# Eight neighbour subtractions from VectorE to GpSimd, and a new order of the engines, in an attention and channel-mix kernel

## The chip, the core and the metric

The kernel runs on one core of a Trainium2 chip. A core has five engines that work at the same time, each through its own list of instructions in order: TensorE (PE, matrix products into the accumulation memory PSUM), VectorE (DVE), ScalarE (ACT), GpSimd (POOL) and SyncE (SP, which here only issues transfers). PEld is the load of weights into TensorE. Engines wait for each other through semaphores. Transfers (DMA) between the main memory and the core's working memory SBUF are issued by POOL, SP or ACT and run on 16 DMA engines.

The metric is the device time of one execution in microseconds (us), the median of several runs.

## The reference

Two stages follow each other. The first is attention with a sliding window of 128 positions and a bias that falls with distance, for 8 batches, 8 heads, 576 positions and head size 64. The second is a channel mix in which each token is blended with its neighbour to the left:

```python
rel = pos[:, None] - pos[None, :]
mask = (rel >= 0) & (rel < 128)
scores = np.where(mask, scale * q @ k.T + bias, -1e9)
attn = softmax(scores);  x = attn @ v           # heads side by side: (8, 576, 512)

x_prev = x shifted by one position, 0 at the start
xk = mu_k * x + (1 - mu_k) * x_prev
xr = mu_r * x + (1 - mu_r) * x_prev
k = np.maximum(xk @ w_k, 0)                     # 512 -> 1024
v = k * k @ w_v                                 # 1024 -> 512
r = 1 / (1 + np.exp(-(xr @ w_r)))               # 512 -> 512
out = r * v
```

The kernel computes xk as mu_k * (x - x_prev) + x_prev, and xr likewise with mu_r. The subtraction x - x_prev is the neighbour-token subtraction.

## The kernel before, in words

**Attention.** Batches come one after the other, and each batch has four groups g of two heads. Batch 0 is treated apart and in two parts (positions 0 to 255 and 256 to 575), so that the channel mix can begin early. Later batches are loaded with q and k in a form that VectorE transposes (line 1157, into qt); TensorE makes the scores on 32-row tiles (line 1190), ScalarE the exponential (line 1211), VectorE multiplies by the mask (line 1224), and TensorE multiplies by v (line 803). VectorE takes the reciprocal of the sums (line 809) and scales (line 814, into xu). The result is turned so that channels lie on partitions: for batches 0 to 3 by TensorE (line 841) with a copy on ScalarE (line 717, into xt), for batches 4 to 7 by a transposing transfer from SP (`out_flip`).

**The shift.** The function `shift` works on xt, which has zeros ahead of the first column, so that the neighbour is the same tile one column to the left. For each batch and group it puts three instructions on VectorE: the subtraction into dl (line 867), then two mixes on line 874, which multiply dl by mu and add the neighbour, into xk and xr. There are two dl buffers, so at most two subtractions are open at a time. The first part of batch 0 uses other buffers and lets its xr come later (argument `late`).

**The channel mix.** Two batches form a pair P of 1152 columns, cut into pieces of 256, 256, 384 and 256 columns (first pair) or 512, 384 and 256. For each piece TensorE makes xk @ w_k (line 956), ScalarE the relu (line 963), ScalarE or VectorE the square (lines 927 and 929), TensorE xr @ w_r (line 974), ScalarE a tanh that stands for the sigmoid (line 981), TensorE kk @ w_v (line 990), and VectorE the final product into ot (line 995). A piece needs xk of all four groups of its columns.

**Loads.** Nearly all loads are issued by POOL, in one fixed order: v, weights, the rest of batch 0, batch 1, then batches 2 to 7 (raw for q and k on line 568, vs and tv for v on lines 547 and 552). POOL computes only an iota, two selects and two tiny copies (lines 481, 489, 492, 660).

**What sets the order.** The program is first built as a graph of nodes, each with an engine, a cost in us and the nodes that it waits for. `Plan.run` then plays the graph through: whenever an engine is free, it takes the ready node with the smallest key. The sequence that comes out is the order in which each engine's instructions are written down, and the chip follows it whatever the real durations are. The function `rank` makes the keys: a node of attention gets (4 * batch + group) * 4.7, one of the channel mix the TensorE time planned ahead of it, and both get an offset from the table NUDGE, which has a number for about a thousand nodes, by the order in which they were created. DMA issues have their own number as key and are chained to the issue before. Operations with two possible engines (a square, for one) go to whichever is free first in the plan. The cost of a subtraction in the plan is `dve_t(n, 2)`, (n/2 + 66)/960 us for n columns.

Of the kernel before, what the change touches and what calls it, by code (L numbers as in the profile page):

```python
# [182 lines left out]
def kernel(  # L183
# [12 lines left out]
    nc = tc.nc  # L196
# [26 lines left out]
    BIAS = ()  # L223
    FIN = 384
# [102 lines left out]
    def dve_t(n, fast=1):  # L327
        return (n / fast + 66) / 960.0
# [103 lines left out]
    def rank(prio, need, free):  # L432
        nudge = NUDGE.get(len(plan.nodes), 0.0)
        if prio[0] == 0:
            _, b, part, g = prio[:4]
# [860 lines left out]
```

## Time and profile before

| | |
|---|---|
| median of 3 runs | 227.17 us (226.61 to 227.76) |
| the profiled execution | 226.8 us |
| its span, from the first to the last instruction | 225.0 us |
| PE busy | 215.5 us (96%) |
| VectorE busy | 195.3 us (87%) |
| ScalarE busy | 167.9 us (75%) |
| GpSimd busy | 58.5 us (26%) |
| subtractions of 128x256, 128x320 and 128x576 | 4, 4 and 28, of 290, 318 and 448 ns |
| granted TensorE clock | 0.999 |

Busy time is the time in which an engine had an instruction under way. TensorE's matmuls are pipelined and their ends are modelled, so 96% does not mean that it ran at its peak. An instruction's duration is from its start to its end, and on VectorE the next one often starts before that end; the distance between starts is then the better measure of what an instruction takes from the engine. A chain that ended last is followed back from the last instruction: at each step to what released it, or to the instruction ahead of it on its engine.

### The profile page before, as it was taken

The numbers are of one execution on the slowest core, as the hardware profiler recorded it, in microseconds if no ns is written. First come the engines' busy times: TensorE is split into PE (matmuls) and PEld (weight loads), VectorE is DVE, ScalarE is ACT, GpSimd is POOL, SyncE is SP. The second block draws the span as 40 slices with busy tenths as digits, with TensorE's granted clock in tenths as the row PEclk, the third lists the DMA queues.
The fourth block names the chain that finished last, engine by engine and source line by source line (L and its number), as shares of the span: only waits on it lengthen the run. The fifth ranks groups of instructions, "written<-read, shape, count | busy, mean of one in ns | idle before, by whom it ended". The sixth has DMA issues, their size and how long they took to land.

```text
span 225.0 us, 5805 instructions
## 1 busy us (share of the span) xinstructions
PE 215.5 (96%) x2309; PEld 128.5 (57%) x2339; DVE 195.3 (87%) x378; ACT 167.9 (75%) x319; POOL 58.5 (26%) x88
## 2 busy tenths in 40 slices
PE   8999978999999999999999999999999999999994
PEld 8575736656755555464774545445674455456642
DVE  7387999999999999999998999999999966993432
ACT  3669999498998689967996997676996884527511
POOL 8758535456101900070005600190000000000000
PEclk9999999999999999999999999999999999999999
DMA  6999999999981996189354993599871315141023
GB/s 162 187 166 200 195 155 207 191 189 188 232 166 50 97 209 154 50 56 145 115 69 45 249 188 84 134 153 186 151 108 29 144 47 117 33 144 62 0 93 140
DMA packets 66298, 29.74 MB, mean 132 GB/s; under 512 B 53976, under 2 KB 58336, under 8 KB 66272
## 3 DMA queue, kind: packets, MB, share of 16 engines
q0 software_dynamic: 46832, 16.26, 66.6%
q1 hardware_dynamic: 17696, 12.53, 19.9%
q10 hardware_dynamic: 1744, 0.59, 1.1%
q8 instruction: 18, 0.29, 0.5%
q14 instruction: 8, 0.07, 0.1%
HBM read 33.56 MB, written 9.44 MB: 191 GB/s over the span
## 4 chain that ended last, share of the span: by engine, by line
PE 88%; DVE 3%; ACT 3%; DMA 3%; issue 1%; SPq 1%; DVEq 0%; ACTq 0%
PE uno L990 27%; PE uno L956 27%; PE uno L974 13%; PE duo L803 7%; PE duo L1190 6%; DMA qx<-in_q_dram 3%; PE uno L841 2%; PE uno L708 1%; PE duo L734 1%; PE uno L803 1%; DVE qt L1157 1%; PE duo L747 1%; SPq L581 1%; ACT rl L963 1%; DVE xk L874 1%
## 5 line engine op out<-in xcount | busy, mean ns | idle before, releaser
L956 PE MATMUL uno<-xk,wk_sb 128*128 128x256 bf16 (+2 forms) x410 | 70.4, 313 | 1.2 <-ACT rs L981 0.3
L990 PE MATMUL uno<-wv_sb,kk 128*128 128x512 bf16 (+2 forms) x281 | 67.1, 373 | 1.2 <-issue 0.6
L1211 ACT ACTIVATE at<-duo 128x1024 bf16<-128x1024 f32 x56 | 55.2, 1040 | 13.6 <-PE duo L1190 13.5
L963 ACT ACTIVATE rl<-uno 128x256 bf16<-128x256 f32 (+2 forms) x104 | 47.0, 478 | 12.2 <-PE uno L956 10.9
L956 PEld LDWEIGHTS <-wk_sb 128*128 128x128 bf16 x416 | 38.8, 98 | 22.8 <-issue 1.8
L990 PEld LDWEIGHTS <-kk 128*128 128x128 bf16 x296 | 27.0, 98 | 29.9 <-issue 2.3
L1224 DVE TENSOR_TENSOR at<-at,mask 128x1024 bf16<-128x1024 bf16 x56 | 37.1, 685 | 1.4 <-ACT at L1211 1.2
L547 POOL DMA_DIRECT2D vs<-in_v_dram x32 | 28.5, 905 | 36.4 <-PE duo L803 29.0
L974 PE MATMUL uno<-wr_sb,xr 128*128 128x512 bf16 x135 | 35.1, 379 | 0.5
L927 ACT ACTIVATE kk<-rl 128x256 bf16<-128x256 bf16 (+2 forms) x74 | 35.1, 517 | 0.5
L1157 DVE STREAM_TRANSPOSE qt<-raw 128x576 f32<-128x576 f32 x28 | 33.4, 1236 | 0.0
L981 ACT ACTIVATE rs<-uno 128x512 bf16<-128x512 f32 x36 | 21.6, 616 | 14.0 <-PE uno L974 13.9
L995 DVE SCALAR_TENSOR_TENSOR ot<-rs,uno 128x512 f32<-128x512 bf16 (+2 forms) x37 | 24.2, 664 | 7.6 <-ACT rs L981 4.6
L874 DVE SCALAR_TENSOR_TENSOR xr<-dl,mu_sb,xt 128x576 bf16<-128x576 bf16 (+1 forms) x32 | 24.6, 771 | 0.1
L874 DVE SCALAR_TENSOR_TENSOR xk<-dl,mu_sb,xt 128x576 bf16<-128x576 bf16 (+1 forms) x32 | 24.5, 776 | 0.1
L803 PEld LDWEIGHTS <-at 128*128 128x128 bf16 x576 | 21.4, 98 | 4.9 <-issue 0.8
L814 DVE TENSOR_TENSOR xu<-duo,rc 128x640 bf16<-128x640 f32 x28 | 22.7, 817 | 0.5 <-PE uno L841 0.3
L974 PEld LDWEIGHTS <-xr 128*128 128x128 bf16 x144 | 13.5, 98 | 14.5 <-issue 0.4
L1190 PE MATMUL duo<-qt 32*128 32x256 bf16 (+2 forms) x560 | 18.1, 250 | 1.1 <-ACT at L1211 0.9
L803 PE MATMUL duo<-vs,at 128*128 128x65 bf16 x448 | 18.8, 194 | 0.3 <-ACT at L1211 0.3
L1190 PEld LDWEIGHTS <-qt 32*128 32x128 bf16 x560 | 11.7, 92 | 11.7 <-issue 9.4
L929 DVE TENSOR_TENSOR kk<-rl 128x256 bf16<-128x256 bf16 (+2 forms) x30 | 10.0, 337 | 8.5 <-ACT rl L963 8.0
(73 smaller groups left out, 159.6 us busy)
## 6 DMA issues: line engine op xcount, KB each, us to landing
out_dram<-ot SPq DMA_DIRECT2D x34, 256.0 KB, 2.5
vs<-in_v_dram POOLq DMA_DIRECT2D x32, 128.0 KB, 9.5
raw<-in_q_dram POOLq DMA_DIRECT2D x14, 288.0 KB, 8.8
raw<-in_k_dram POOLq DMA_DIRECT2D x14, 288.0 KB, 9.3
wk_sb<-in_moe_w_k_dram POOLq DMA_DIRECT2D x2, 512.0 KB, 7.8
wv_sb<-in_moe_w_v_dram POOLq DMA_DIRECT2D x2, 512.0 KB, 11.5
qx<-in_k_dram ACTq DMA_DIRECT2D x4, 128.0 KB, 5.1
qx<-in_q_dram SPq DMA_DIRECT2D x4, 128.0 KB, 4.8
```

What stands on the lines that cost most here:

```text
L547: return dma(POOL, 256, issue_t(1024), lambda e: nc.gpsimd.dma_start(out=vs_buf[h.idx][:, j, :, 0:D], in_=v[b, :, 128 * j:128 * j + 128].r ...
L803: nc.tensor.matmul(a[:, hl, t - t0], lhsT=at[:, lo:lo + 128], rhs=vs[:, u, 2 * g + hl, :] if u < NF else tvb[:, 2 * g + hl], start=(u == u ...
L874: lambda e: nc.vector.scalar_tensor_tensor(out=buf[hk.idx][:, g, e0 + c0:e0 + c1], in0=dls(), scalar=mu[:, g:g + 1], in1=xc(1), op0=ALU.mu ...
L927: nc.scalar.activation(out=out, in_=in_, func=AF.Square)
L956: nc.tensor.matmul(one(hp)[:, 0:n], lhsT=wk_sb[:, po, 128 * fo:128 * fo + 128], rhs=xk_buf[hx.idx][:, po, c0:c1], start=(po == 0), stop=(p ...
L963: a = op(ACT, act_t(n), [s], pr, lambda e, hp=hp, hr=hr: nc.scalar.activation(out=rl_buf[hr.idx][:, 0:n], in_=one(hp)[:, 0:n], func=AF.Rel ...
L974: nc.tensor.matmul(one(hp), lhsT=xr_buf[hx.idx][:, po, 128 * c:128 * c + 128], rhs=wr_sb[:, po], start=(po == 0), stop=(po == NPO - 1))
L990: nc.tensor.matmul(one(hv)[:, a:b], lhsT=kk_buf[hk.idx][:, fo, o:o + 128], rhs=wv_sb[:, fo, a:b], start=(fo == 0), stop=(fo == NFO - 1))
L1157: nc.vector.transpose(out=qt_buf[hq.idx][:, S * i:S * i + S].rearrange("p s t -> p (s t)").bitcast(FP32) .rearrange("p (q t) -> p t q", t=TB),
L1190: nc.tensor.matmul(two(hps[j // 2])[:, j % 2, c0:c0 + n], lhsT=qt[r:r + 32, S + 128 * u:S + 128 * u + 128, t], rhs=qt[r:r + 32, q0:q0 + n, t],
L1211: lambda e, ah=ah, j=j: nc.scalar.activation(out=ah(), in_=two(hps[j]), func=AF.Exp, scale=float(scale)), (), [hps[j]])
L1224: nc.vector.tensor_tensor(out=a, in0=a, in1=m, op=ALU.mult)
```

## The change

The subtraction gets a choice of engine. For the second part of batch 0 (four groups of 320 columns) and for batch 1 (four groups of 576 columns) it goes to GpSimd, with a planned cost of 0.0016 us for a column and 0.2 us more. The first part of batch 0 and batches 2 to 7 stay on VectorE. The keys that `rank` gives now include one for GpSimd, equal to TensorE's. The table NUDGE is another one from end to end, with about as many entries, so the order on every engine, and the engine of the squares, can differ throughout.

```diff
+    XPOOL = (0, 1)
...
     NUDGE = {
-        647: 9.44, 648: 14.18, 650: 28.28, 651: -0.02, 652: 28.26, 654: 14.18, 655: 14.18, 656: -0.02, 657: 4.7, 658: 23.5, 659: 14.12, 660: 9.48,
...
+        1914: 2.42, 1916: 1.54, 1918: 18.57, 1923: 0.24, 1925: 18.1,
     }
...
-    def rank(prio, need, free):
+    def keys_of(prio, need, free):
         nudge = NUDGE.get(len(plan.nodes), 0.0)
...
         return {e: (1e9,) + tuple(prio) for e in LEAD}
+
+    def rank(prio, need, free):
+        d = keys_of(prio, need, free)
+        d[POOL] = d[PE]
+        return d
...
         prev = last.get(("xt", b, g))
         last["xt", b, g] = deps[0]
-        d = op(DVE, dve_t(n, 2), list(deps) + [prev], prio + (1, 0),
-               lambda e: nc.vector.tensor_tensor(
+        on = POOL if late is None and b in XPOOL else DVE
+        d = op(on, 0.0016 * n + 0.2 if on == POOL else dve_t(n, 2), list(deps) + [prev], prio + (1, 0),
+               lambda e: (nc.gpsimd if on == POOL else nc.vector).tensor_tensor(
             out=dls(), in0=xc(0), in1=xc(1), op=ALU.subtract), [hd], [ht])
```

148 rows, old and new, of the table NUDGE are left out of this document.

## The prediction

> **What bounds the kernel now.** I read the page of the profile first (shares and the chain), then the table by stretches of 7.5 us, then the chain in order of time, then the groups by shape.
>
> ```profile
> span 225.0 us, 5805 instructions
> PE 215.5 (96%) x2309; PEld 128.5 (57%) x2339; DVE 195.3 (87%) x378; ACT 167.9 (75%) x319; POOL 58.5 (26%) x88
> PE 88%; DVE 3%; ACT 3%; DMA 3%; issue 1%; SPq 1%; DVEq 0%; ACTq 0%
> ```
>
> TensorE is the bound over the whole span, and VectorE holds only 3% of the chain that ended last, about 7 us. Those 7 us have a place. In the next table the columns are the stretch, its length, then for each engine busy us and instructions, the granted clock, the DMA share and GB/s.
>
> ```profile
> 15.00:22.50 7.50, 6.79 (x142) 4.05 (x142) 6.23 (x19) 7.15 (x21) 4.71 (x8) 1.00 1.51 188
> 22.50:30.00 7.50, 6.97 (x108) 4.99 (x107) 7.36 (x16) 7.41 (x18) 3.47 (x5) 1.00 1.49 187
> 30.00:37.50 7.50, 6.13 (x89) 4.10 (x90) 7.50 (x15) 7.43 (x15) 3.87 (x6) 1.00 1.79 178
> 37.50:45.00 7.50, 7.11 (x104) 4.90 (x105) 7.13 (x17) 4.51 (x10) 3.58 (x6) 1.00 1.42 196
> 45.00:52.50 7.50, 7.45 (x80) 4.22 (x80) 7.50 (x12) 5.88 (x11) 4.49 (x6) 1.00 1.71 194
> 52.50:60.00 7.50, 7.50 (x81) 5.29 (x79) 7.43 (x14) 7.50 (x21) 1.87 (x4) 1.00 1.78 208
> 105.00:112.50 7.50, 7.40 (x109) 5.10 (x110) 7.50 (x16) 7.32 (x16) 0.00 (x0) 1.00 0.28 91
> ```
>
> From 15 to 45 us PE is idle for 0.71 + 0.53 + 1.37 + 0.39 = 3.0 us, and VectorE is full from 22.5 us on, ScalarE from 15 to 37.5 us. In the three later rows PE has at most 0.10 us idle, although VectorE stays full. So a microsecond of VectorE is worth something to the end only between about 22 and 45 us, and afterwards only where a VectorE result arrives just in time.
>
> The chain in order of time (start, length, what) shows that stretch:
>
> ```profile
> 27.99 1.02 DVE xu L814 x2
> 29.25 1.17 DVE qt L1157
> ...
> 31.34 0.68 DVE at L1224
> 32.02 1.17 DVE qt L1157
> 33.34 0.45 DVE xr L874
> 33.79 0.94 DVE xk L874 x2
> 34.77 0.83 PE uno L956 x6
> ```
>
> From 27.99 to 34.77 us the chain runs on VectorE nearly without a break and ends in the last xk of batch 0, for which the matmuls of line 956 wait. The break before 33.34 is the subtraction's (33.03 us, below).
>
> **The change part by part.** *Part 1, removed from VectorE.* The eight subtractions that move are the four of 128x320 and the first four of 128x576 on line 867. VectorE's timeline (start, length) has them here:
>
> ```profile
> 24.12 0.33 DVE L867 TENSOR_TENSOR dl<-xt 128x320 bf16<-128x320 bf16 x1
> 24.48 0.55 DVE L874 SCALAR_TENSOR_TENSOR xr<-dl,mu_sb,xt 128x320 bf16<-128x320 bf16 x1
> 33.03 0.31 DVE L867 TENSOR_TENSOR dl<-xt 128x320 bf16<-128x320 bf16 x1
> 33.27 0.52 DVE L874 SCALAR_TENSOR_TENSOR xr<-dl,mu_sb,xt 128x320 bf16<-128x320 bf16 x1
> 43.79 0.44 DVE L867 TENSOR_TENSOR dl<-xt 128x576 bf16<-128x576 bf16 x1
> 44.15 0.82 DVE L814 TENSOR_TENSOR xu<-duo,rc 128x640 bf16<-128x640 f32 x1
> 50.25 0.82 DVE L867 TENSOR_TENSOR dl<-xt 128x576 bf16<-128x576 bf16 x2
> 50.99 1.54 DVE L874 SCALAR_TENSOR_TENSOR xk<-dl,mu_sb,xt 128x576 bf16<-128x576 bf16 x2
> ```
>
> Instructions overlap their neighbour, so what one costs is the distance to the next start: 0.36 us at 24.12, 0.24 us at 33.03, 0.36 us at 43.79, and 0.37 us each for the two at 50.25. I take 0.27 us for each small one (4 x 0.27 = 1.1 us, between 24 and 33.3 us, in the starved stretch) and 0.37 us for each large one (4 x 0.37 = 1.5 us, between 43.8 and 51 us). Of the 1.1 us I count 0.8: ScalarE is as full there (7.41 and 7.43 of 7.5 us) and takes a part of the bound. Ends: 0 and 1.1. Of the 1.5 us I count 0.5. Line 956 turns to batch 1 at 52.59 us, right behind the last xk at 50.99 + 1.54 = 52.53 us, so VectorE is just in time there, but PE shows no wait. Ends: 0 and 1.5.
>
> ```profile
> 52.59 3.52 PE L956 MATMUL uno<-xk,wk_sb 128*128 128x384 bf16 x24
> ```
>
> *Part 2, added to GpSimd.* No two-input operation of GpSimd is in the trace. The nearest rows are these (busy us, mean ns):
>
> ```profile
> L492 POOL TENSOR_SCALAR_AFFINE_SELECT dist<-dist 128x128 bf16<-128x128 bf16 x1 | 0.4, 367 | 0.0
> L660 POOL COPY gap<-xt 1x4 bf16<-1x4 bf16 x2 | 0.4, 178 | 37.5 <-DMA xt<-xu 37.5
> L481 POOL IOTA dist<- 128x256 bf16 x1 | 0.3, 344 | 0.4 <-POOLq L1280 0.4
> ```
>
> Between the copy of 4 elements (178 ns) and the select of 128 (367 ns) lie 1.5 ns for an element. That gives 0.65 us for 320 elements and 1.04 us for 576, in all 6.8 us. Ends: the iota's slope, (344 - 178)/252 = 0.66 ns, gives 0.39 and 0.56 us, in all 3.8 us; twice the select's slope, because there are two inputs, gives 1.1 and 1.9 us, in all 12 us. I take the middle, since the select is the nearest in kind. GpSimd has 2.8 to 4 us idle in each of the stretches concerned, so the work fits. [...]
>
> *Part 3, the new waits.* GpSimd's queue now waits for ScalarE's copy of xt, and behind it stand DMA issues; VectorE's xr and xk now wait for GpSimd. A ready subtraction goes ahead of a ready DMA issue in the planner's order, as its key is smaller. The tightest transfer is the last raw load of batch 2:
>
> ```profile
> 34.44 0.53 POOL L568 DMA_DIRECT2D raw<-in_k_dram  x1 [0.86 <-PE duo L1190]
> 44.89 1.25 DVE L1157 STREAM_TRANSPOSE qt<-raw 128x576 f32<-128x576 f32 x1
> raw<-in_k_dram POOLq DMA_DIRECT2D x14, 288.0 KB, 9.3
> ```
>
> Issued at 34.44 and landing 9.3 us later, it is there at 43.7 us, 1.1 us before the first transpose of that batch at 44.89 us. The four small subtractions put 2.6 us into GpSimd's queue before it. The queue idles 0.86 us before this issue and as long before most others, so I count nothing; if that cover fails, the transpose starts up to 1.5 us late. One subtraction is slower by 0.65 - 0.27 = 0.4 us in its own path to xr and xk, but starts as soon as xt is there rather than behind other VectorE work (the one at 33.03 had waited behind a transpose): nothing counted.
>
> *Part 4, the two engines disturb each other.* The trace shows GpSimd holding VectorE up in one place:
>
> ```profile
> 2.22 1.96 POOL L547 DMA_DIRECT2D vs<-in_v_dram  x2
> L687 DVE COPY dist<-dist 128x192 bf16<-128x192 bf16 x1 | 0.6, 620 | 0.0
> L687 DVE COPY dist<-dist 128x64 bf16<-128x64 bf16 x1 | 0.5, 524 | 0.0
> L687 DVE COPY dist<-dist 128x256 bf16<-128x256 bf16 x1 | 0.2, 214 | 0.0
> L1224 DVE TENSOR_TENSOR at<-at,mask x56: 666/684/693, 31.3 to 183.4; 128x1024 bf16<-128x1024 bf16 x56
> L874 DVE SCALAR_TENSOR_TENSOR xr<-dl,mu_sb,xt x32: 521/812/819, 24.5 to 199.7; 128x576 bf16<-128x576 bf16 x28, 128x320 bf16<-128x320 bf16 x4
> 22.50:45.00 22.50, 3.93 (x8) 1.00 1.57 187
> 22.50:45.00 22.50, 5.16 (x8) 1.00 1.57 187
> ```
>
> Copies of 192 and 64 columns took 620 and 524 ns while a GpSimd instruction ran, although 256 columns take 214 ns. The mask products of line 1224 have two inputs in SBUF and never took more than 693 ns, but GpSimd had only DMA issues then. So the price of a GpSimd subtraction to VectorE is unknown: at the low end 0, at the high end its whole duration. The last two rows are VectorE's busy time from 22.5 to 45 us on line 874 and on line 1224 alone: operations with two SBUF inputs fill (3.93 + 5.16)/22.5 = 40% of it. With an operation hit at a random moment of the 0.65 us, the delay is about 0.15 us each, 0.6 us for the four in the starved stretch. I take 0.6; the ends are 0 and 2.6 us.
>
> *Part 5, the new order.* The table NUDGE is other throughout, so every engine's list changes. What it can gain is what PE idles: of the 3.0 us, parts 1 and 4 leave 2.5. What it can lose has no row of its own; the bound is to pay the starved stretch's largest idle, 1.37 us, once more in a place that is now dense, with some loss in the small gaps: 2 us. I take a gain of 0.7, under a third of what is left, because VectorE and ScalarE are both full there and reordering moves, but doesn't remove, their work. Ends: 2.5 gained, 2 lost.
>
> **Sum.** 0.8 + 0.5 - 0.6 + 0.7 = 1.4 us gained. The profiled execution took 226.8 us (span 225.0), so 225.4 by its own time; the median of the three runs is 227.17, 0.4 above it: 225.8 us. Ends by the terms: 1.1 + 1.5 + 2.5 = 5.1 gained, or 2.6 + 1.5 + 2 = 6.1 lost.
>
> **The rivals.** *Slower: GpSimd holds VectorE for its whole duration.* Place: the stretch from 24 to 35 us, and 43 to 52 us. Each subtraction then takes 0.65 or 1.04 us from VectorE where it took 0.27 or 0.37. The four small ones lose 2.6 - 1.1 = 1.5 us in the starved stretch, the large ones 4.2 - 1.5 = 2.7 us, of which a third, as in part 1, reaches PE: 0.9. Without a gain by order: 227.17 + 2.4 = 229.6; with it 228.9. It decides from a delay of 0.27 us for each small one. For it: the copies above. Against it: the other operations had no such row. [...] The stretched copies agree with a lock, at 620 and 524 ns; for two-input operations no row here tests it.)
>
> *Slower: the order packs PE worse after 45 us.* The idle there is at most 0.10 us in the rows shown, so it has more to lose than to gain; a loss of 1.4 to 2 us eats the gain of part 1: 227.9 to 228.5.
>
> *No change: PE sets the end anyway.* If the relieved time of VectorE is taken by ScalarE's fullness, or given back as waits in the dense part, the time is 227.2.
>
> *Much faster: the order fills the starved stretch.* All of 3.0 us idle and 0.5 of part 1: 223.7.
>
> **How the numbers follow.** Forecast (225.8, its own range 224.8 to 226.0) 0.34; much faster 0.12; no change 0.20; the lock 0.20; the worse order 0.14. A time within 0.5% (1.1 us) of before is about what a measurement can't tell from no change: faster 0.46, same 0.20, slower 0.34. The range reaches from 222.8, the fast case with one more of part 1's microseconds, to 229.7, which takes in the lock's case at the middle price; the longer subtractions (12 us in all) lie beyond it.
>
> **What would show it.** Part 1: 24 subtractions of 128x576 left on VectorE and none of 128x320. Part 2: GpSimd rows on line 867's successor near 0.65 and 1.04 us. Part 4: xr, xk and at rows whose longest is far above 819 and 693 ns, each beside a GpSimd subtraction. Part 5: PE's busy time from 15 to 45 us above 27.0 of 30 us, and from 45 us on as dense as now. Part 3: a wait of qt for a raw load near 44 us, or of xk for GpSimd. The forecast is wrong if the starved stretch doesn't get denser, or if it does and the dense part loses as much.

## The result, and the profile after

The changed kernel takes 245.24 us (median of 4 runs, 244.53 to 246.23) where the kernel before takes 227.12 us (4 runs, 226.61 to 227.76). The ratio is 1.080, with a 95% interval of 1.077 to 1.084: 18.1 us slower, where 1.4 us faster was forecast and the range ended at 229.7 us.

The head of its page and the shares of its chain:

```profile
span 244.4 us, 5821 instructions
PE 219.6 (90%) x2309; PEld 130.6 (53%) x2339; DVE 202.4 (83%) x390; ACT 162.1 (66%) x299; POOL 67.2 (28%) x96
...
PE 71%; DMA 15%; DVE 7%; issue 3%; ACT 3%; POOL 1%; DVEq 0%; POOLq 0%; ACTq 0%; SPq 0%
```

TensorE's share of the chain fell from 88% to 71%, and transfers rose from 3% to 15%. GpSimd itself holds 1%. The table by stretches (columns as in the prediction) has the place:

```profile
15.00:22.50 7.50, 7.20 (x140) 4.24 (x128) 6.40 (x20) 7.22 (x19) 4.81 (x8) 1.00 1.64 179
22.50:30.00 7.50, 5.39 (x95) 4.20 (x94) 4.49 (x9) 7.29 (x18) 3.80 (x5) 1.00 1.47 194
30.00:37.50 7.50, 0.06 (x1) 0.06 (x2) 1.14 (x3) 0.00 (x0) 4.72 (x8) 0.52 1.85 180
37.50:45.00 7.50, 4.83 (x62) 2.73 (x67) 5.79 (x10) 5.81 (x8) 4.86 (x7) 0.79 1.41 196
45.00:52.50 7.50, 4.18 (x53) 2.93 (x43) 5.29 (x11) 3.12 (x5) 1.79 (x3) 0.66 1.77 175
52.50:60.00 7.50, 7.45 (x94) 5.47 (x93) 5.74 (x10) 3.83 (x10) 1.15 (x1) 0.88 0.25 64
```

From 30 to 37.5 us TensorE, VectorE and ScalarE all stand nearly still. TensorE's busy time times its clock, as a rough measure of its progress, is 13.2 us between 30 and 60 us (0.06 x 0.52 + 4.83 x 0.79 + 4.18 x 0.66 + 7.45 x 0.88), against 28.2 us before. With the two rows above (0.4 us gained, then 1.6 us lost) that is 16.2 of the 19.4 us by which the span grew. The table of waits (engine, tile, line, what released it: us in total, times, longest) names the chain of causes:

```profile
DVE xk L875 <- POOL dl L868: 12.1, 3, 8.7
PE uno L841 <- DVE xu L814: 9.5, 1, 9.5
```

VectorE's mix xk waits 8.7 us in one piece for a subtraction, and TensorE 9.5 us for the xu that stands behind that wait in VectorE's list. VectorE's timeline and TensorE's first row after the gap:

```profile
27.36 0.27 DVE L809 RECIPROCAL rc<-uno 128x6 f32<-128x6 f32 x2
36.37 0.55 DVE L875 SCALAR_TENSOR_TENSOR xk<-dl,mu_sb,xt 128x320 bf16<-128x320 bf16 x1 [8.73 <-POOL dl L868]
36.84 0.55 DVE L814 TENSOR_TENSOR xu<-uno,rc 128x384 bf16<-128x384 f32 x1
...
37.44 0.50 PE L841 MATMUL uno<-ident,xu 128*128 128x128 bf16 x3 [9.52 <-DVE xu L814]
```

Why was the subtraction so late? Two of them run together at 34.93 us, and this xk needs the second, which ends at 34.93 + 1.40 = 36.33 us. Their operands, ScalarE's copies into xt, were there at 24.5 and 26.7 us, 10 and 9 us before they ran. ScalarE's rows, and then GpSimd's timeline, which answers (the bracket is the idle time before, and what ended it):

```profile
24.08 0.42 ACT L717 COPY xt<-uno 128x320 bf16<-128x320 bf16 x1
...
26.23 0.46 ACT L717 COPY xt<-uno 128x320 bf16<-128x320 bf16 x1
```

```profile
19.09 0.75 POOL L572 DMA_DIRECT2D wr_sb<-in_moe_w_r_dram  x1 [0.69 <-DMA vs<-in_v_dram]
20.01 1.77 POOL L547 DMA_DIRECT2D vs<-in_v_dram  x2 [0.18 <-issue]
22.35 0.88 POOL L547 DMA_DIRECT2D vs<-in_v_dram  x1 [0.57 <-DMA wk_sb<-in_moe_w_k_dram]
23.75 0.88 POOL L547 DMA_DIRECT2D vs<-in_v_dram  x1 [0.53 <-DMA raw<-in_q_dram]
25.40 0.70 POOL L552 DMA_DIRECT2D tv<-in_v_dram  x1 [0.78 <-DMA raw<-in_k_dram]
26.60 0.76 POOL L572 DMA_DIRECT2D wv_sb<-in_moe_w_v_dram  x1 [0.50 <-DMA raw<-in_q_dram]
27.97 0.74 POOL L572 DMA_DIRECT2D wv_sb<-in_moe_w_v_dram  x1 [0.60 <-DMA raw<-in_k_dram]
30.77 0.54 POOL L568 DMA_DIRECT2D raw<-in_q_dram  x1 [2.06 <-DMA wr_sb<-in_moe_w_r_dram]
31.95 0.54 POOL L568 DMA_DIRECT2D raw<-in_k_dram  x1 [0.63 <-DMA vs<-in_v_dram]
32.83 0.53 POOL L568 DMA_DIRECT2D raw<-in_q_dram  x1 [0.35 <-DMA vs<-in_v_dram]
34.38 0.53 POOL L568 DMA_DIRECT2D raw<-in_k_dram  x1 [1.01 <-DMA vs<-in_v_dram]
34.93 1.40 POOL L868 TENSOR_TENSOR dl<-xt 128x320 bf16<-128x320 bf16 x2
```

Count back from the issue at 30.77: the issue eight places earlier is that of wr_sb at 19.09, and its landing, 11.1 us after the issue and so at 30.2 us, is what the wait ended with. The next three wait for vs loads, again eight places back. In this trace no issue on GpSimd's queue starts before the eighth issue ahead of it has landed (71 of its 79 issues have eight ahead of them). The kernel's own plan knows nothing of that: it starts the four raw issues between 22.2 and 23.9 us and the first two subtractions at 24.5 and 26.7 us, and so they are written behind them. On the chip the first ran at 34.93 us, 10.4 us later than planned. In the kernel before the same queue was as late (the prediction shows its last raw issue at 34.44 us), but it carried only loads there, and no engine's result.

### The profile page after: what moved, and what is told of

The parts are those of the page before. It is cut to its first block, busy times and chain, and to the rows that moved or that the text cites. A ratio compares the mean times of both kernels' runs of the same rounds, so it can differ in the third digit from the quotient of the medians.

```text
span 244.4 us, 5821 instructions
## 1 busy us (share of the span) xinstructions
PE 219.6 (90%) x2309; PEld 130.6 (53%) x2339; DVE 202.4 (83%) x390; ACT 162.1 (66%) x299; POOL 67.2 (28%) x96
## 3 DMA queue, kind: packets, MB, share of 16 engines
q1 hardware_dynamic: 17696, 12.53, 18.1%
## 4 chain that ended last, share of the span: by engine, by line
PE 71%; DMA 15%; DVE 7%; issue 3%; ACT 3%; POOL 1%; DVEq 0%; POOLq 0%; ACTq 0%; SPq 0%
PE uno L991 23%; PE uno L957 21%; PE uno L975 11%; PE duo L803 6%; PE duo L1191 5%; DMA vs<-in_v_dram 5%; DMA raw<-in_k_dram 5%; DMA wk_sb<-in_moe_w_k_dram 3%; PE uno L708 2%; DMA xt<-xu 2%; DVE xk L875 2%; DVE xu L814 1%; PE uno L841 1%; DVE ot L996 1%; DVE qt L1158 1%
## 5 line engine op out<-in xcount | busy, mean ns | idle before, releaser
L957 PE MATMUL uno<-xk,wk_sb 128*128 128x256 bf16 (+2 forms) x413 | 71.8, 315 | 4.4 <-DVE xk L875 3.3
L991 PE MATMUL uno<-wv_sb,kk 128*128 128x512 bf16 (+2 forms) x280 | 68.1, 376 | 1.5 <-issue 1.0
L957 PEld LDWEIGHTS <-wk_sb 128*128 128x128 bf16 x416 | 38.8, 98 | 28.2 <-issue 6.3
L1225 DVE TENSOR_TENSOR at<-at,mask 128x1024 bf16<-128x1024 bf16 x56 | 38.0, 698 | 0.3
L975 PE MATMUL uno<-wr_sb,xr 128*128 128x512 bf16 x133 | 36.3, 385 | 0.8 <-issue 0.2
L875 DVE SCALAR_TENSOR_TENSOR xk<-dl,mu_sb,xt 128x576 bf16<-128x576 bf16 (+1 forms) x32 | 25.7, 802 | 12.3 <-POOL dl L868 12.1
L928 ACT ACTIVATE kk<-rl 128x256 bf16<-128x256 bf16 (+2 forms) x59 | 27.5, 495 | 0.4
L803 PEld LDWEIGHTS <-at 128*128 128x128 bf16 x576 | 22.3, 100 | 6.3 <-issue 2.8
L930 DVE TENSOR_TENSOR kk<-rl 128x256 bf16<-128x256 bf16 (+2 forms) x45 | 15.2, 347 | 10.0 <-ACT rl L964 9.7
L717 ACT COPY xt<-uno 128x576 bf16<-128x576 bf16 (+2 forms) x20 | 10.8, 544 | 16.7 <-PE uno L841 16.7
L803 PE MATMUL duo<-vs,at 128*128 128x65 bf16 x448 | 19.6, 197 | 1.4 <-DVE xu L814 1.2
```

Of the source, the lines that this page charges most:

```text
L803: nc.tensor.matmul(a[:, hl, t - t0], lhsT=at[:, lo:lo + 128], rhs=vs[:, u, 2 * g + hl, :] if u < NF else tvb[:, 2 * g + hl], start=(u == u ...
L875: lambda e: nc.vector.scalar_tensor_tensor(out=buf[hk.idx][:, g, e0 + c0:e0 + c1], in0=dls(), scalar=mu[:, g:g + 1], in1=xc(1), op0=ALU.mu ...
L928: nc.scalar.activation(out=out, in_=in_, func=AF.Square)
L957: nc.tensor.matmul(one(hp)[:, 0:n], lhsT=wk_sb[:, po, 128 * fo:128 * fo + 128], rhs=xk_buf[hx.idx][:, po, c0:c1], start=(po == 0), stop=(p ...
L975: nc.tensor.matmul(one(hp), lhsT=xr_buf[hx.idx][:, po, 128 * c:128 * c + 128], rhs=wr_sb[:, po], start=(po == 0), stop=(po == NPO - 1))
L991: nc.tensor.matmul(one(hv)[:, a:b], lhsT=kk_buf[hk.idx][:, fo, o:o + 128], rhs=wv_sb[:, fo, a:b], start=(fo == 0), stop=(fo == NFO - 1))
```

## The experiments

The theory: the subtractions stand in GpSimd's list behind issues that wait for landings, and what waits for them stands in order on VectorE and TensorE. The rivals: the new order alone; the lock between GpSimd and VectorE; the clock, which is 0.52 in the idle stretch; GpSimd's longer operations. Beside these runs the kernel before took 226.6 to 226.7 us; the ratios are against it.

**The order and the engine apart.** The new order with the subtractions issued on VectorE:

```diff
-               lambda e: (nc.gpsimd if on == POOL else nc.vector).tensor_tensor(
+               lambda e: nc.vector.tensor_tensor(
```

> The new order kept on every engine, only the eight subtractions run on VectorE, at the place in the order that the plan gave them. Theory 1, the queue: the time went because a subtraction stands on GpSimd behind transfer issues that wait, and VectorE and then TensorE wait for it; then 227 to 231 us, with no idle stretch of TensorE near 30 to 37 us. Rival, the order: the new table is bad by itself; then 240 us or more. Rival, the lock (a GpSimd subtraction holds VectorE up for its whole duration): the lock goes too, so this run reads like theory 1; the next two tell them apart.

Measured: 232.54 us, ratio 1.027 (1.023 to 1.031), 1.5 us above what was expected if the queue were the whole cause, and far below the 240 us of the order as the cause. So 5.9 us are lost by the order without any work on GpSimd. By busy time times clock TensorE is 2.6 us behind the kernel before at 37.5 us, 3.7 at 60, 4.0 at 165 and 4.9 at 172.5. Most of it falls in the starved stretch, which the new order made worse; here TensorE waits for ScalarE's exponentials (what held these up was not followed):

```profile
30.00:37.50 7.50, 4.60 (x76) 2.92 (x77) 7.50 (x15) 5.96 (x10) 3.62 (x6) 0.88 1.88 180
...
PE duo L1191 <- ACT at L1212: 3.6, 2, 2.5
```

And the order before, with the eight subtractions on GpSimd at their old places:

```diff
-               lambda e: nc.vector.tensor_tensor(
+               lambda e: (nc.gpsimd if late is None and b < 2 else nc.vector).tensor_tensor(
```

> The order of before kept on every engine, only the eight subtractions run on GpSimd, at the place in the order where they were. Theory 1, the queue: the first subtraction, with its xt ready near 24 us, stands behind two or three raw issues of batch 2, which went out from 30.6 us on, and VectorE waits about 7 to 9 us for it at 24.5 us; 236 to 245 us. Rival, the order: 226 to 228 us. Rival, the lock: the eight subtractions cost about 1 us each where they meet an operation with two SBUF inputs, less 2.5 us saved; 228 to 231 us.

Measured: 241.77 us, 1.066 (1.063 to 1.069). The engine alone costs 15 us in the old order, and 245.24 - 232.54 = 12.7 us in the new one (12.1 by the ratios, since the kernel before took 227.12 us on the one occasion and 226.61 on the other). So 5.9 and 15 us do not add up to 18.1 us. Both fall in the same stretch, which would explain it; that was not shown.

**One instruction.** Of the eight, only the first 128x320 one goes to GpSimd, in the old order (node 730 is its number in the plan):

```diff
-               lambda e: nc.vector.tensor_tensor(
+               lambda e: (nc.gpsimd if e == POOL else nc.vector).tensor_tensor(
...
-                n.emit(n.eng)
+                n.emit(POOL if n.seq == 730 else n.eng)
```

> The kernel before, with one instruction moved: the first subtraction of 128x320 (xt ready near 24 us) runs on GpSimd, at its old place in the order, which is behind three raw issues of batch 2; no other subtraction moves. Theory, the queue: it runs near 33.6 us, VectorE stands at the mix behind it from about 24.5 us, and this one instruction of 0.3 us costs 7 to 10 us: 234 to 237 us. Rival, the lock: at most 1 us: 226 to 228 us.

Measured: 238.61 us, 1.053 (1.048 to 1.058), 1.6 us above the expected range. One instruction, which ran 0.73 us, costs 12 us. GpSimd, and then VectorE:

```profile
32.77 0.53 POOL L568 DMA_DIRECT2D raw<-in_q_dram  x1 [0.86 <-DMA vs<-in_v_dram]
33.31 0.73 POOL L867 TENSOR_TENSOR dl<-xt 128x320 bf16<-128x320 bf16 x1
...
34.08 0.55 DVE L874 SCALAR_TENSOR_TENSOR xr<-dl,mu_sb,xt 128x320 bf16<-128x320 bf16 x1 [10.55 <-POOL dl L867]
```

A wait of 10.55 us is 14 times the 0.73 us that the instruction ran, so neither its duration nor VectorE held for all of that duration makes it up. The xr that stood at 24.48 us in the kernel before now starts at 34.08 us.

The four of batch 1 alone, in the old order:

```diff
-               lambda e: nc.vector.tensor_tensor(
+               lambda e: (nc.gpsimd if b == 1 else nc.vector).tensor_tensor(
```

> The kernel before, with only the four subtractions of batch 1 on GpSimd, at their old places in the order. There the first stands behind a vs issue that went out at 48.45 us, its xt ready at 43.8 us, its mix due at 47.4 us. Theory, the queue: a wait of 2 to 4 us on VectorE, partly covered by TensorE's other work: 227.5 to 231 us. Rival, the lock: four times 0.9 us on VectorE, less 1.5 us saved: 227 to 229 us; it is told by mixes and mask products of 1.6 us or more without an idle VectorE.

Measured: 235.12 us, 1.037 (1.033 to 1.042), 4 us above the expected range. It is the same kind of wait at another place, behind loads of v:

```profile
49.08 0.89 POOL L547 DMA_DIRECT2D vs<-in_v_dram  x1 [1.18 <-DMA vs<-in_v_dram]
...
52.89 1.17 POOL L867 TENSOR_TENSOR dl<-xt 128x576 bf16<-128x576 bf16 x1
...
54.09 0.82 DVE L874 SCALAR_TENSOR_TENSOR xr<-dl,mu_sb,xt 128x576 bf16<-128x576 bf16 x1 [7.49 <-POOL dl L867]
```

The xr that waits needs the second of the four subtractions, at 52.89 us. Ahead of it stand the v issue at 49.08 us, the first subtraction at 49.99 us and two more v issues at 51.08 us, which take 1.80 us without an idle gap. So a part of this wait is the time that the issues themselves take, and not a landing.

**The subtractions ahead of the issues.** In the changed kernel the loads of wv_sb, of v for batch 2 and of raw for batches 2 and 3 are written behind subtractions of batch 0, and nothing else is touched. The numbers are nodes of the plan: 190 and 202 load wv_sb, 215 to 236 raw for batch 2, 244 to 264 v for batch 2, and 269 to 290 raw for batch 3; 715, 760 and 745 are subtractions of batch 0.

```diff
-        for n in plan.run():
+        todo = plan.run()
+        for after, moved in ((715, (190, 202)), (760, (215, 222, 229, 236)), (745, (244, 249, 254, 259, 264, 269, 276, 283, 290))):
+            late_ = [n for n in todo if n.seq in moved and n.eng == POOL]
+            todo = [n for n in todo if n not in late_]
+            at = [n.seq for n in todo].index(after) + 1
+            todo[at:at] = late_
+        for n in todo:
```

> The changed kernel, with the transfer issues of wv, of batch 2 and the raw ones of batch 3 put behind the small subtractions on GpSimd's queue; all else, the engine of the subtractions too, as in the changed kernel. Theory 1, the queue: the first two subtractions run near 26 us, VectorE's wait of 8.7 us goes; 227 to 233 us. Rival, the order: 240 us or more. Rival, the lock: 4 to 6 us above the run with the subtractions on VectorE.

Measured: 235.48 us, 1.040 (1.037 to 1.043). That is 2.5 us above the expected range, but 9.8 us of the 12.7 come back by order on one queue alone. The first two subtractions run at 26.12 us instead of 34.93:

```profile
26.12 1.40 POOL L868 TENSOR_TENSOR dl<-xt 128x320 bf16<-128x320 bf16 x2
...
DVE xr L875 <- POOL dl L868: 3.2, 1, 3.2
```

The same in the old order, with all eight subtractions on GpSimd (the loop as above, other places; 298 to 318 load v for batch 3, and 889, 909 and 917 are subtractions of batch 1):

```diff
+        for after, moved in ((730, (190, 202)), (760, (215, 222, 229, 236, 244, 249, 254, 259, 264)), (889, (276,)), (909, (283, 290, 298, 303)), (917, (308, 313, 318))):
```

> The order of before on TensorE, VectorE and ScalarE, all eight subtractions on GpSimd, and the transfer issues of wv, of batch 2 and batch 3 put behind them so that none waits in the queue. Theory, the queue: the 15 us of the run with the engine alone go for the most part; the issues are 1 to 2 us late and the lock costs VectorE 2 to 4 us, less 2.5 us saved: 226 to 230 us. If moving the subtraction is worth something by itself, this is below 226.6 us. Rival, that the wait isn't the queue's but GpSimd's latency: above 235 us.

Measured: 230.99 us, 1.019 (1.015 to 1.022), 10.8 us below the kernel with the engine alone and 1 us above the expected range. It stays above the kernel before. Two things seen in its trace can be the reason, and were not taken apart: the first subtraction still waits behind v loads (VectorE idles 2.40 us for it), and the raw loads of batch 2 are issued 2 to 4 us later. And with only the last two subtractions of batch 0 on GpSimd, the raw and v issues of batch 2 behind them:

```diff
+    TWO = ((0, 256, 2), (0, 256, 3))
...
+               lambda e: (nc.gpsimd if (b, c0, g) in TWO else nc.vector).tensor_tensor(
...
+        for after, moved in ((760, (215, 222, 229, 236, 244, 249, 254, 259, 264)),):
```

> The kernel before, with only the last two subtractions of batch 0 on GpSimd, and the raw and v issues of batch 2 put behind them. Their xt is ready at 30.8 to 31.2 us, GpSimd is idle then, and VectorE is full. Does a moved subtraction pay where nothing stands before it: VectorE saves 2 x 0.24 = 0.5 us and the lock meets an operation with two inputs about once, 0.4 us; the raw issues go out 1.5 us later. 226 to 228 us; below 226.2 us it would beat both kernels.

Measured: 227.32 us over 12 runs, 1.004 (1.002 to 1.006). VectorE waits for no subtraction here, and relieving it in the starved stretch brings nothing that outweighs the rest (the first raw issue of batch 2 starts 2 us later): the gain of part 1 was not found.

**The lock by itself.** In the kernel before, ten two-input subtractions of 128x576 and then ten memsets are added to GpSimd at 152 us, where its queue is empty. They write a tile that nobody reads any more.

```diff
+                    nc.gpsimd.tensor_tensor(out=junk, in0=wk_sb[:, 0, 0:576], in1=wk_sb[:, 1, 0:576],
+                                            op=ALU.subtract)
...
+                    nc.gpsimd.memset(junk, 0.0)
```

> The kernel before, with ten more subtractions of 128x576 from constants and then ten memsets of 128x576 on GpSimd, written to a tile that nobody reads, from about 153 us on when GpSimd has nothing else to do; nothing waits for them. Theory, the lock: mask products and mixes that begin during a GpSimd subtraction last 1.3 to 1.7 us instead of 0.68 and 0.81, VectorE loses about 0.5 us for each subtraction, and GpSimd's own take 1.1 to 1.9 us; during the memsets nothing is stretched. The time: VectorE is full there, TensorE just covered, so 227 to 232 us. Rival, no lock: 226.6 us and no row above 0.83 us.

Measured: 231.55 us, 1.022 (1.019 to 1.024). The added group, and VectorE beside it:

```profile
L1269 POOL TENSOR_TENSOR sid<-wk_sb x10: 1283/1600/1677, 152.3 to 166.8; 128x576 bf16<-128x576 bf16 x10
...
151.34 2.94 DVE L874 SCALAR_TENSOR_TENSOR xk<-dl,mu_sb,xt 128x576 bf16<-128x576 bf16 x1
154.21 1.82 DVE L874 SCALAR_TENSOR_TENSOR xr<-dl,mu_sb,xt 128x576 bf16<-128x576 bf16 x1
155.96 0.67 DVE L995 SCALAR_TENSOR_TENSOR ot<-rs,uno 128x512 f32<-128x512 bf16 x1
...
159.38 3.43 DVE L1224 TENSOR_TENSOR at<-at,mask 128x1024 bf16<-128x1024 bf16 x2
162.74 2.32 DVE L1157 STREAM_TRANSPOSE qt<-raw 128x576 f32<-128x576 f32 x2
...
169.19 0.68 DVE L1224 TENSOR_TENSOR at<-at,mask 128x1024 bf16<-128x1024 bf16 x1
```

A mix that takes 0.81 us elsewhere took 2.94 and 1.82 us, two mask products 3.43 us instead of 0.68 each. Another mask product and another mix took 1.16 and 1.22 us, so such an operation lost between 0.4 and 2.1 us. The product of line 995, which has only one input in SBUF, kept its 0.67 us, the transposes their 1.16 to 1.23 us, and the mask product at 169.19 us, beside the memsets (168.1 to 174.4 us), its 0.68 us. Why the first mix, which begins a microsecond ahead of the first added row, lost more than one subtraction takes, stays open. So these subtractions did hold VectorE up, and with them and the memsets, in a dense stretch, the kernel took 231.55 - 226.7 = 4.9 us more. In the changed kernel it shows too (a mix of 1.69 us at 63.10), but the single subtraction and the queue put in another order give most of the engine's loss to the wait.

**The clock.** In the changed kernel 150 matmuls on a tile of zeros fill the gap before the transposes that waited; their result is overwritten.

```diff
+            if n.seq == 758:
+                for i in range(150):
+                    nc.tensor.matmul(one(n.need[0])[:, 0:128], lhsT=warm, rhs=warm, start=True, stop=True)
```

> The changed kernel, with 150 small matmuls on zeros put into TensorE's list just ahead of the transposes that waited from 27.9 to 37.4 us; their results are overwritten. In the changed kernel the granted clock was 0.52 to 0.88 from 30 to 60 us. If the lowered clock after the idle stretch costs time of its own: the windows' busy time times (1 - clock) gives 4.83 x 0.21 + 4.18 x 0.34 + 7.45 x 0.12 = 3.3 us, so 242 us at a clock of 1.0. If VectorE and GpSimd set the pace until 60 us anyway: 245 us, at a clock of 1.0.

Measured: 245.07 us, 1.081 (1.078 to 1.085), no change, although the clock was 0.99 to 1.00 from 22.5 to 45 us:

```profile
30.00:37.50 7.50, 7.28 (x130) 7.04 (x126) 1.31 (x3) 0.55 (x1) 4.89 (x8) 1.00 1.83 181
...
45.00:52.50 7.50, 3.10 (x26) 2.28 (x27) 5.23 (x12) 2.70 (x5) 1.96 (x4) 0.50 1.77 177
```

In this kernel TensorE idles 4.31 us for an xk before 49.18 us, and the clock of the stretch from 45 to 52.5 us is 0.50; in the changed kernel it was 0.52 in the stretch with the gap of 9.5 us. How the clock depends on the idle time was not taken apart. The clock in the first gap is not what sets the time: the later subtractions still came when GpSimd's queue let them, at 42.76 and 47.81 us against 42.48 and 47.46. But the expectation spoke of a clock of 1.0 up to 60 us, and that was not reached. What the lowered clock of the second gap costs is neither shown nor ruled out; by busy time times the missing share of the clock from 45 to 60 us it would be some 3 us (3.10 x 0.50 + 7.45 x 0.17).

**The plan told of the queue.** If the cause is that the plan doesn't know the wait, a plan that does should put the subtractions right. In the changed kernel, the nodes of GpSimd's issues also wait for the landing of the eighth issue before:

```diff
-        n = plan.add(queue, issue, 0.0, list(deps) + [last.get(queue)],
+        back = landed[-8:-7] if queue == POOL else []
+        n = plan.add(queue, issue, 0.0, list(deps) + [last.get(queue)] + back,
...
+            landed.append(x)
```

> The changed kernel, with one wait added to the plan from which the order is made: each transfer issue on GpSimd waits for the landing of the eighth issue before it. Nothing else is edited; the order that comes out is another one. In the trace of before, the raw issue at 30.58 us waits for the landing of wr_sb, which is the eighth issue before it. Theory, the queue: with that wait the plan puts the subtractions where they are ready in time, VectorE's wait of 8.7 us goes, and the time falls to 229 to 236 us, as in the run with the issues put behind. Rival, that the waits of the issues come from elsewhere: the subtractions are late again, 240 us or more.

Measured: 265.81 us, 1.173 (1.169 to 1.176): a miss by 30 us. But the queue began as planned: the plan has the first two subtractions at 24.6 and 26.7 us and the first raw load of batch 2 at 30.8, and the chip has

```profile
24.62 0.72 POOL L874 TENSOR_TENSOR dl<-xt 128x320 bf16<-128x320 bf16 x1 [0.34 <-ACT xt L723]
...
26.80 0.72 POOL L874 TENSOR_TENSOR dl<-xt 128x320 bf16<-128x320 bf16 x1 [0.80 <-ACT xt L723]
...
30.32 0.54 POOL L574 DMA_DIRECT2D raw<-in_q_dram  x1 [1.31 <-DMA wr_sb<-in_moe_w_r_dram]
...
DVE xk L881 <- POOL dl L874: 0.6, 1, 0.6
...
165.00:195.00 30.00, 18.31 (x229) 11.38 (x224) 22.95 (x42) 8.95 (x10) 2.53 (x5) 0.68 0.29 71
```

Further on the chip falls behind this plan: the first subtraction of batch 1 is planned at 47.2 us and started at 50.12. But VectorE's waits for subtractions are down to 0.6 us. The time is lost elsewhere, above all at 165 to 195 us, where TensorE is idle for 11.7 us. The numbers of NUDGE had been chosen for a plan without the wait, and in this one they do harm: this plan's own end is 249.6 us, against 223.5 us of the plan they were made for. I had left that out of the expectation. So the keys were searched anew for the plan with the wait (FIX holds the new offset of each node), and the same order was also run with the subtractions on VectorE:

```diff
+    FIX = {
...
+    for n in plan.nodes:
+        if n.seq in FIX:
+            n.prio = {e: (k[0] + FIX[n.seq],) + tuple(k[1:]) for e, k in n.prio.items()}
```

> The changed kernel with two things in the plan: GpSimd's issues wait for the landing of the eighth issue before, as in queue_in_plan, and the keys are searched anew for that plan (by the planned end alone, 250 to 223 us; the kernel before has 221.3 in the same plan and takes 227.1). The subtractions are planned at 26.2, 27.7, 33.5 and 34.8 us, and the four of batch 1 from 45.2 to 51 us. If the queue is the cause of the loss: they run within 1 us of those times, VectorE and TensorE together wait less than 3 us for them up to 60 us, and the time is the plan's end with the offset of the kernel before, 223.2 + 5.8 = 229 us (227 to 233). If GpSimd's work as such is the cause (the lock, or its durations), the time stays above 236 us although the subtractions are on time.

> The same order as queue_searched, with the eight subtractions issued on VectorE. It shows what the move of the engine costs once the order knows the queue. If GpSimd costs little then: within 2 us of queue_searched, on either side. If the lock or the handing over between engines weighs: 3 us or more below it. If VectorE's relief in the starved stretch is worth what was predicted: 1 to 2 us above it.

Measured: 234.80 us with the subtractions on GpSimd, 1.037 (1.032 to 1.041), and 235.48 us with them on VectorE, 1.038 (1.033 to 1.042). The first, on GpSimd, has them at

```profile
26.18 0.72 POOL L874 TENSOR_TENSOR dl<-xt 128x320 bf16<-128x320 bf16 x1 [0.26 <-ACT xt L723]
...
27.66 0.73 POOL L874 TENSOR_TENSOR dl<-xt 128x320 bf16<-128x320 bf16 x1
...
L881 DVE SCALAR_TENSOR_TENSOR xk<-dl,mu_sb,xt x32: 521/812/1701, 30.9 to 206.3; 128x576 bf16<-128x576 bf16 x28, 128x320 bf16<-128x320 bf16 x4
```

Planned were 26.2 and 27.7 us, and VectorE shows no wait for GpSimd up to 60 us. The move of the engine, which cost 12.7 and 15 us where the plan didn't know the queue, costs nothing that can be measured where it does (the two differ by 0.7 us, and the times of each spread over 2 us), though mixes are still stretched to 1.70 us. What VectorE is relieved of may cancel what it loses; that was not taken apart. The time itself was expected at 227 to 233 us and missed: both kernels stay 8 to 9 us above the kernel before, and since the one without GpSimd's work does too, that part is the order's. Why this order's time lies 234.8 - 223.2 = 11.6 us above its plan's end, and that of the kernel before only 226.6 - 221.3 = 5.3 us, stays open.

## Why the prediction was wrong

**The step that failed is part 3, the new waits.** It asked what the subtractions delay in GpSimd's queue, and answered "nothing", as the queue idles before most issues. The row it rested on was the answer to the other question: an issue that idles 0.86 us before it starts is an issue that waits, and everything written behind it waits too. The sentence that the subtraction "starts as soon as xt is there ... nothing counted" is the term that was off: the first two started 10 and 9 us after their xt was there. Its ground, that a ready subtraction goes ahead of a ready issue, holds in the plan, where the four raw issues are over by 24.5 us; on the chip they stood ahead of it until 34.9 us. Moving the engine cost 12.7 us in the new order and 15 us in the old one, and 9.8 and 10.8 us of these came back by the order of GpSimd's queue alone, where zero was written; what the rest consists of was not taken apart. The rows that would have shown it stood in the trace of before: raw issues from 30.58 to 34.44 us, and an xr at 24.48 us. The first of the issues, with its wait:

```profile
30.58 0.54 POOL L568 DMA_DIRECT2D raw<-in_q_dram  x1 [2.11 <-DMA wr_sb<-in_moe_w_r_dram]
```

All the ends of the prediction's sum together come to 6.1 us lost, so no choice within them reaches 18.1 us.

**Part 5, the order,** has the wrong sign: 5.9 us lost where 0.7 were to be gained and 2 lost was the end. The bound was too narrow: the starved stretch itself got worse (by 3.0 us at its end, by the busy time times clock), and single stretches late in the kernel lost up to 0.85 us. The rival with the worse order looked only behind 45 us.

**Part 1, VectorE's relief.** A gain of 0.8 + 0.5 us was counted. It was not found: two subtractions moved without waits came out 0.4% slower. The pair with a good place in the queue came out 0.7 us apart, in favour of GpSimd but within the spread of the runs, so a gain of this size is not ruled out there.

**Part 2, GpSimd's durations,** had 0.65 and 1.04 us. By shape the changed kernel shows 730 and 1251 ns: a little low, and not where the time went.

```profile
L868 POOL TENSOR_TENSOR dl<-xt 128x320 bf16<-128x320 bf16 x4 | 2.9, 730 | 0.0
L868 POOL TENSOR_TENSOR dl<-xt 128x576 bf16<-128x576 bf16 x4 | 5.0, 1251 | 8.8 <-ACT xt L717 8.1 <-DVE xr L875 0.7
```

**Part 4, the lock,** asked about a hold-up that the runs show (a mix of 2.94 us beside the added subtractions, 0.81 us elsewhere), and its size was not far off. That the operations with two SBUF inputs are the ones hit was the author's estimate there; beside the added subtractions mixes and mask products were stretched, and the products of line 995 were not (0.67 us). Ten added subtractions, 15.0 us long in all, cost 4.9 us together with the memsets behind them, about a third of their duration, where the prediction took 0.15 of 0.65 us, just under a quarter. As the rival it was priced at 2.4 us at most, and it does not carry the result. The list of signs did name the one that came, "a wait ... of xk for GpSimd", but no rival had that wait with a price: the forecast went wrong because it was looked for at 44 us, at a transfer, and not at 24 us, at the subtraction.

## What to carry to other kernels

Before compute is put on a queue that issues transfers, read that queue's timeline and ask when the instruction ahead of it is really done: an idle time before an issue is a wait that the new work inherits, and the engines that need its result inherit it in turn (here the first two subtractions ran 10 and 9 us after their operands were there, and VectorE waited 8.7 us). An order written by a plan is only as good as the waits that the plan knows; compare planned with measured start times on every queue, above all on one that nobody depended on so far. Offsets chosen for one plan can do harm in another (265.81 us here), so an engine and an order should be judged apart.

## What the runs showed of the hardware

In the trace of the changed kernel no issue on GpSimd's queue starts before the eighth issue ahead of it has landed (the one at 30.77 us, whose eighth landed at 30.2). With that wait in the plan, planned and measured starts agreed within 0.5 us in the two rows of subtractions and the one of a raw load shown where the plan was first told of the queue (24.62, 26.80 and 30.32 us for 24.6, 26.7 and 30.8). Whether the program or the queue makes this wait was not tried.

Beside GpSimd's added memsets a mask product kept its 0.68 us, while beside the added subtractions a mix took 2.94 us, where one takes 0.81 us elsewhere. That came as the expectation of that run had it, but for the size: it had 1.3 to 1.7 us.
